# Chunk 4's scores in two steps, and the last weight pieces as halves through the scalar engine's queue: a fused attention and expert kernel on one Trainium2 core

## The chip, the cores and the metric

The kernel runs on one core of a Trainium2 chip. The core has a matrix engine (TensorE, PE in the rows), a vector engine (VectorE, DVE), a scalar engine (ScalarE, ACT), GpSimd (POOL), and a synchronisation engine (SyncE, SP) that here only starts transfers. ScalarE can start transfers as well. Each engine works through its own list of instructions in the order in which that list was written, and waits at the head of the list until what the instruction needs is there. The list of transfers that an engine starts is called its queue in this text. The metric is the time of one execution on the device in microseconds (us). Before the change it is 1141.03 us, the median of three runs (1140.71 to 1143.52).

## The reference, cut to what matters

Eight sequences of 576 tokens with 8 heads of 64 go through block-causal attention, and its output (4608 tokens by 512) through a two-layer expert with a gate. All is in float32; the two weight matrices come as 64-bit floats.

```python
scores = scale * np.matmul(q, k.transpose(0, 1, 3, 2))
mask = block_i >= block_j            # blocks of 64 positions
scores = np.where(mask, scores, -1000000000.0)
attn = np.exp(scores - np.max(scores, axis=-1, keepdims=True))
attn = attn / (np.sum(attn, axis=-1, keepdims=True) + 1e-09)
x = np.matmul(attn, v)               # then heads side by side: 4608 x 512
h = x @ w_in                         # 512 x 2048
g = h * (1.0 / (1.0 + np.exp(-1.702 * h)))
return (g @ w_out).astype(np.float32)   # 2048 x 512
```

## The kernel before, in words

**Turns.** Two heads make a pair, and 32 pairs give 32 turns, n = 0 to 31, and a last one. A turn scores pair n, multiplies pair n-1's weights with its values, and prepares pair n+1. The 576 rows of a pair are cut into five chunks, 0 to 4; chunk i has 64(2i+1) keys, so that chunk 4 is the widest with 576. What a turn does, and in which order, is written as a string of slots (lines 29 to 33, read by `order` and `step`). "3+0" scores chunks 3 and 0 side by side, "2+1" the next two, "4" the last. "V" multiplies the turned weights of the pair before with its values (`av`). "L" is `prep`: VectorE turns the loaded q and k of the next pair, and the loads for the pair behind that go out. B, C and a flip weights by TensorE in the first five turns only. After each slot, "-" too, weights are converted up to a quota and expert work goes out up to another quota. Turns 0 to 3 use FIRST, turn 4 START, turn 5 HANDOVER, turns 6 to 8 CONVERT and all later ones LATE.

**A pair's way.** `score` issues one product per chunk and head into a PSUM bank. `weigh` takes the bank with VectorE (line 349: mask, scale and row minimum in one instruction) and then ScalarE (line 356: the exponential with its sum). `normalise` makes the reciprocal on VectorE (lines 366 and 369) and scales the row on GpSimd (line 374). From turn 5 on `turn` transposes 32 by 32 blocks on VectorE into the tile `turned` (lines 383 and 388), and behind chunk 4 sixteen transfers on SP's queue (line 395) carry the blocks to the other partitions, from where `av` reads them. There is one copy of the source blocks and one of the target blocks: the next pair's transposes wait until the sixteen transfers have read, and the transfers wait until `av` has read.

**Banks.** [...] `bank` goes round the banks w0, w1 and w2 once the experts have begun, and from turn 9 on w3 as well. "3+0", "2+1" and "V" take two banks each. The order of TensorE's products is that of the source.

**Experts.** Tiles of 384 tokens go through 16 column groups fc of the hidden layer: 12 products into `hp`, the gate (lines 555, 556, 564 and 79), then 9 products of the group before into three accumulators. Tile 0 starts in turn 4, and its fc = 0 to 15 call for the weights as they go.

**Weights.** The 64-bit weights are split into a high and a low float32 part. There are 32 pieces of 128 rows by 512: for each of four column groups g, four pieces of w_in and then four of w_out. `load_weights` fetches a piece; `begin` turns the upper word by a ScalarE instruction into the bank w3 (line 213); `merge` takes the lower word on VectorE (lines 226 and 229) into `wm`, of which there is one; `split_weights` casts the high part on ScalarE (line 238) and subtracts on GpSimd (line 79). The first 28 pieces land in rooms that final weights will fill later. For the last four, all of w_out's group 3, no such room is left: each lands as two halves in the three buffers of the tag `osb`, which the output tiles use afterwards. `convert` runs a piece in two steps, `merge`, then `split_weights` and the next `begin`. The quota follows `WEIGHTS_BY` (position: pieces; position counts heads, two a turn), and the expert calls for a piece itself where the quota lags.

**Order.** All of this is the source's order. A planner reads it as priorities and writes each engine's list by its own estimate of durations; only TensorE's products and the first three weight loads are held to the order of the source.

The lines that the prediction's steps touch: 31 and 32 (the orders of turns 5 to 8), 36 (the quota), 184 to 202 (`load_weights`; its transfers all go through SP's queue, line 195), 208 to 239 (`begin`, `merge`, `split_weights`), 241 to 256 (`convert`), 303 to 336 (`score`), 395 (the sixteen transfers), 427 to 452 (`av`), and 536 (the expert's call for pieces).

Of the kernel before, what the change touches and what calls it, by code (L numbers as in the profile page):

```python
# [27 lines left out]

FIRST = "1+0 - B 2/3 - L C - 4 - V - a -"
START = "1+0 - B 2/3 C - V - 4 - a - L -"  # L30
HANDOVER = "B - C - 3+0 - V - 2+1 - - 4 - - L -"
CONVERT = "3+0 - 2+1 - - V - 4 - - - L - -"
LATE = "3+0/2+1 - - - - V - 4 - - - L -"


WEIGHTS_BY = ((0, 0), (8, 13), (14.5, 32))
TILES_BY = ((8.4, 0), (17, 1), (33.7, 4), (65.7, -2))


# [1 line left out]
def attention_moe_kernel(  # L41
# [29 lines left out]
    def f(ap):  # L71
        return ap.bitcast(F32)
# [38 lines left out]
    WC = 512  # L111
    NG = DF // WC
    FG = WC // P
    GROUP = NDC + FG

    def room(tag, shape, dt, name):
        return d2.tile(shape, dt, tag=tag, name=name, bufs=1)
# [44 lines left out]
    def width(i):  # L162
        return BLK * (2 * i + 1)
# [9 lines left out]
    for g in range(NG):  # L173
        for dc in range(NDC):
            src = wi64[dc * P : (dc + 1) * P, 2 * g * WC : 2 * (g + 1) * WC]
            pieces.append((src, "wi", g, dc))
        for fc in range(FG):
            r = (g * FG + fc) * P
            pieces.append((wo64[r : r + P], "wo", g, fc))

    places = [f"{n}{p}{g}" for n, g in (("wo", 3), ("wo", 2), ("wi", 3), ("wi", 2), ("wo", 3), ("wi", 3), ("wo", 3)) for p in "hl"]
    parts, pair_of = {}, {}

    def load_weights(upto):
        while conv["loaded"] < min(upto, len(pieces)):
            j = conv["loaded"]
            if j < 2 * len(places):
                if j % 2 == 0:
                    pair_of[j // 2] = room(places[j // 2], [P, 2, 2 * WC], U32, "words")
                at = [pair_of[j // 2][:, j % 2]]  # L190
            else:
                at = [d2.tile([P, WC], U32, tag="osb", name="wst", bufs=3) for _ in range(2)]
            n = 2 * WC // len(at)
            for x, w in enumerate(at):
                d = nc.sync.dma_start(out=w, in_=pieces[j][0][:, x * n : (x + 1) * n])
                if j < 3:
                    tc.keep_in_program_order(d)
            parts[j] = [
                (w.rearrange("p (c t) -> p c t", t=2), slice(x * n // 2, (x + 1) * n // 2))
                for x, w in enumerate(at)  # L200
            ]
            conv["loaded"] += 1


# [3 lines left out]
    def begin(j):  # L208


        bits[j] = ps.tile([P, 512], F32, tag="w3", name="wm")
        for w, c in parts[j]:
            nc.scalar.activation(
                out=bits[j][:, c], in_=f(w[..., 1]), func=AF.Prelu, scale=2.0**-112, alpha=-(2.0**32)
            )

    def merge(j):
        u = bits.pop(j).bitcast(U32)

        if j % 2 and j < 2 * len(places) - 4:  # L220
            z = d2.tile([P, WC], U32, tag="osb", name="wm", bufs=3)
        else:
            z = room("wm", [P, WC], U32, "wm")
        whole[j] = z
        for w, c in parts.pop(j):
            nc.vector.tensor_scalar(
                out=z[:, c], in0=w[..., 0], scalar1=29, scalar2=None, op0=ALU.logical_shift_right
            )
            nc.vector.scalar_tensor_tensor(
                out=z[:, c], in0=u[:, c], scalar=3, in1=z[:, c],  # L230
                op0=ALU.logical_shift_left, op1=ALU.bitwise_or,
            )

    def split_weights(j):
        _, name, g, x = pieces[j]
        z = whole.pop(j)
        hi, lo = (weights(name + p, g)[:, x] for p in "hl")
        nc.scalar.copy(out=hi, in_=f(z))  # L238
        subtract(nc.gpsimd, lo, f(z), f(hi))

    def convert(upto):

        while conv["step"] < int(2 * upto):
            j, odd = divmod(conv["step"], 2)
            if odd:
                split_weights(j)
                if j + 1 < len(pieces):
                    load_weights(min(j + 3, 2 * len(places) + 1))
                    begin(j + 1)
            else:  # L250
                if j == 0:
                    begin(0)
                merge(j)
                if j >= 2 * len(places):
                    load_weights(j + 2)
            conv["step"] += 1


    raw, qk = {}, {}
# [41 lines left out]
    stats = {}  # L301

    def score(n, banks):

        if n not in stats:
            mx = d2.tile([P, NCH + 1, 2], F32, tag="mx", name="mx")
            sm = d2.tile([P, NCH, 2], F32, tag="sm", name="sm")
            stats[n] = (mx, sm)
        todo = []
        for chunks in banks:  # L310

            part = []
            for lo, hi in ((0, 512),) if width(chunks[0]) <= 512 else ((0, 256), (256, S)):
                ss = [bank() for _ in range(2)]
                c = 0
                for i in chunks:
                    a, z = qrange(i)
                    w = min(hi, width(i)) - lo
                    for hd in range(2):
                        r = slice(hd * D, hd * D + D)  # L320

                        mm(
                            out=ss[hd][:, c : c + w], lhsT=qk[n][r, 0, a : a + P],
                            rhs=qk[n][r, 1, lo : lo + w], start=True, stop=True,
                        )
                        part.append((i, hd, lo, lo + w, ss[hd][0 : z - a, c : c + w]))
                    c += w
            todo.append(sorted(part, key=lambda x: (chunks[::-1].index(x[0]), x[2])))
        for chunks, part in zip(banks, todo):
            e = {}  # L330
            for i, hd, lo, hi, s in part:
                e[i] = weigh(n, i, hd, lo, hi, s, e.get(i))
            for i in chunks[::-1]:
                normalise(n, i, e[i])
                if not early(n):
                    turn(n, i, e[i])

    def weigh(n, i, hd, lo, hi, s, e):
        mx, sm = stats[n]
# [22 lines left out]
    def normalise(n, i, e):  # L362
        _, sm = stats[n]
        m = BLK if i == 0 else P
        c = sm[0:m, i]
        nc.vector.tensor_scalar(  # L366
            out=c, in0=c, scalar1=1e-9, scalar2=2.0, op0=ALU.add, op1=ALU.mult
        )
        nc.vector.reciprocal(out=c, in_=c)  # L369
# [94 lines left out]
    def step(n):  # L464

        turns["n"] = n
        now = n < NPAIR

        def item(x):
            if x == "V":  # L470
                return (lambda: av(n - 1)) if n else None
            if x == "L":
                return (lambda: prep(n + 1)) if n + 1 < NPAIR else None
            if x in ("a", "B", "C"):
                m, chunks = {"a": (n, [0, 1]), "B": (n - 1, [2, 3]), "C": (n - 1, [4])}[x]
# [33 lines left out]
    def moe():  # L509
# [17 lines left out]
        for t in range(NT):  # L527
# [5 lines left out]
            acc = [ps.tile([P, DM], F32, tag=f"acc{c}", name=f"acc{c}") for c in range(tt // P)]  # L533
            for fc in range(NFC):
                if t == 0:
                    convert(fc // FG * GROUP + NDC + fc % FG + 1)
                hp = ps.tile([P, 512], F32, tag="h", name="hp")
                fs = slice(fc % FG * P, (fc % FG + 1) * P)
                terms = [(wa, xb, dc) for dc in range(NDC) for wa, xb in (("wih", xh), ("wil", xh), ("wih", xl))]
# [112 lines left out]
```

## Time and profile before

| what | value |
|---|---|
| median of three runs | 1141.03 us (1140.71 to 1143.52) |
| the profiled execution: its own time | 1139.9 us |
| its span, first to last instruction | 1138.1 us (1.8 us of the time lie around it) |
| TensorE busy in the span | 1076.8 us (95%) |
| VectorE, ScalarE, GpSimd busy | 580.2, 487.6, 409.6 us |
| turns 5 to 8 | from about 96 to 234 us of the span |
| TensorE busy from 96 to 234 us | 112.5 of 138 us |
| TensorE busy from 420 to 980 us | about 99% |

In a row of the timeline stand the start, the duration, engine, line, operation, tiles and count, and in brackets the time for which the engine sat idle before it, with what released it. A row of the waits has who waited for whom, then the total, the number of times and the longest. "SPq" is a transfer in SP's queue; its duration is the time it takes to be issued, not to land. PEclk is the clock granted to TensorE in tenths of full speed.

### The profile page before, as it was taken

The page shows a single profiled execution, that of the slowest core. Times are in us where ns is not written, and L with a number is a line of the kernel's source. Part 1 is how long each engine was busy: PE and PEld are TensorE (multiplying, and loading weights), DVE is VectorE, ACT ScalarE, POOL GpSimd, SP SyncE. Part 2 cuts the span into 40 slices and gives each one's busy share as a digit, 9 for nine tenths or more (in the row PEclk, how much of TensorE's full clock was granted, in tenths as well). Part 3 has the DMA queues.
Part 4 walks back from the last instruction along what each step waited for, and adds up shares of the span by engine and source line. Part 5 has one row for each costly group of instructions (what it writes and reads, how often), then busy time and mean ns, then how long its engine had stood idle before and what let it go on. Part 6 is the DMA issues. An engine that isn't in the chain of part 4 may idle for free. (4 is left out here: it accounts for less than half of the span.)

```text
span 1138.1 us, 19868 instructions
## 1 busy us (share of the span) xinstructions
PE 1076.8 (95%) x6870; PEld 910.4 (80%) x6870; DVE 580.2 (51%) x1863; ACT 487.6 (43%) x1291; POOL 409.6 (36%) x509
## 2 busy tenths in 40 slices
PE   5879796899999999999999999999999999999998
PEld 3658574788788888888888888888888888899997
DVE  6766765645555655554555655455555564211211
ACT  5866543533343444443443443343443344232322
POOL 5665644333233333333333233332332333222222
PEclk8979899899999999999999999999999999999999
DMA  8653363443343343343343333343333332200000
GB/s 173 196 143 91 106 174 78 103 102 84 73 101 75 69 99 67 78 112 81 77 106 72 70 90 65 84 111 74 84 97 69 70 90 56 53 29 1 29 1 28
DMA packets 221668, 95.66 MB, mean 84 GB/s; under 512 B 198528, under 2 KB 198528, under 8 KB 221568
## 3 DMA queue, kind: packets, MB, share of 16 engines
q1 hardware_dynamic: 216832, 93.81, 35.0%
q10 hardware_dynamic: 4736, 0.59, 0.3%
q8 instruction: 54, 0.88, 0.3%
q14 instruction: 46, 0.38, 0.1%
HBM read 45.09 MB, written 9.44 MB: 48 GB/s over the span
## 5 line engine op out<-in xcount | busy, mean ns | idle before, releaser
L79 POOL TENSOR_TENSOR gl<-g,gh 128x384 fp32r<-128x384 f32 x192 | 195.3, 1017 | 542.3 <-ACT gh L564 449.6
L96 PE MATMUL hp<-xh,wih 128*128 128x384 f32 x768 | 266.1, 346 | 11.0 <-DVE g L556 10.3
L556 DVE SCALAR_TENSOR_TENSOR g<-g,hp 128x384 f32<-128x384 f32 x192 | 105.6, 550 | 329.6 <-ACT g L555 328.4
L96 PE MATMUL hp<-xh,wil 128*128 128x384 f32 x768 | 260.1, 339 | 0.0
L96 PE MATMUL hp<-xl,wih 128*128 128x384 f32 x768 | 254.8, 339 | 0.0
L555 ACT ACTIVATE g<-hp 128x384 f32<-128x384 f32 x192 | 94.2, 491 | 349.7 <-PE hp L96 343.0
L96 PE MATMUL acc<-woh,gh 128*128 128x512 f32 x576 | 232.6, 404 | 3.5 <-ACT woh L238 3.5
L96 PE MATMUL acc<-wol,gh 128*128 128x512 f32 x576 | 228.7, 397 | 0.6 <-POOL wol L79 0.6
L96 PE MATMUL acc<-woh,gl 128*128 128x512 f32 x576 | 228.0, 396 | 0.5 <-POOL gl L79 0.5
L356 ACT ACTIVATE e<-e,mx 64x64 f32<-64x64 f32 (+1 forms) x270 | 148.9, 553 | 80.1 <-DVE mx L349 80.1
L374 POOL TENSOR_TENSOR e<-e,sm 128x448 f32<-128x448 f32 (+4 forms) x222 | 135.6, 631 | 129.2 <-DVE sm L369 76.0
L96 PEld LDWEIGHTS hp<-xh,wih 128*128 128x128 f32 x768 | 145.5, 189 | 35.4 <-DVE g L556 22.3
L564 ACT CAST gh<-g 128x384 fp32r<-128x384 f32 x192 | 98.5, 513 | 156.1 <-DVE g L556 155.9
L96 PEld LDWEIGHTS hp<-xh,wil 128*128 128x128 f32 x768 | 145.7, 190 | 6.9 <-issue 0.2
L96 PEld LDWEIGHTS hp<-xl,wih 128*128 128x128 f32 x768 | 145.0, 189 | 0.4 <-DVE xl L79 0.4
L96 PE MATMUL bank<-qk 64*128 64x320 f32 (+4 forms) x768 | 123.7, 430 | 20.7 <-DVE mx L349 9.3
L96 PEld LDWEIGHTS acc<-woh,gh 128*128 128x128 f32 x576 | 108.7, 189 | 34.2 <-issue 9.9
L383 DVE STREAM_TRANSPOSE turned<-e 128x384 f32<-128x384 f32 (+1 forms) x216 | 104.4, 500 | 62.0 <-POOL e L374 56.6
L96 PEld LDWEIGHTS acc<-wol,gh 128*128 128x128 f32 x576 | 108.6, 189 | 24.6 <-POOL wol L79 1.1
L96 PEld LDWEIGHTS bank<-qk 64*128 64x128 f32 x768 | 70.6, 194 | 65.0 <-issue 30.1
L96 PEld LDWEIGHTS acc<-woh,gl 128*128 128x128 f32 x576 | 108.8, 189 | 17.2 <-POOL gl L79 1.4
L349 DVE CUSTOM_DVE_ANT_0 e<-bank,mask 64x64 f32<-64x64 f32 (+2 forms) x270 | 99.5, 417 | 29.2 <-PE bank L96 25.6
(48 smaller groups left out, 865.9 us busy)
## 6 DMA issues: line engine op xcount, KB each, us to landing
turned<-turned SPq DMA_DIRECT2D x216, 80.0 KB, 2.1
turned<-turned SPq DMA_DIRECT2D x108, 112.0 KB, 2.2
turned<-turned SPq DMA_DIRECT2D x108, 88.0 KB, 2.1
raw<-in_q_dram SPq DMA_DIRECT2D x128, 72.0 KB, 2.4
out_dram<-osb SPq DMA_DIRECT2D x36, 256.0 KB, 2.3
raw<-in_k_dram SPq DMA_DIRECT2D x120, 72.0 KB, 2.4
words<-in_moe_w_in_dram SPq DMA_DIRECT2D x16, 512.0 KB, 6.3
vp<-in_v_dram SPq DMA_DIRECT2D x60, 128.0 KB, 2.4
```

The source lines that it names most:

```text
L79: eng.tensor_tensor(out=out, in0=in0, in1=in1, op=ALU.subtract)
L96: return tc.keep_in_program_order(nc.tensor.matmul(**kw))
L349: nc.vector.tensor_tensor_reduce(out=e[0:m, hd, lo:hi], in0=s, in1=mk, op0=ALU.add, op1=ALU.min, scale=-0.125, scalar=3e38 if lo == 0 else ...
L356: nc.scalar.activation(out=e[0:m, hd], in_=e[0:m, hd], func=AF.Exp, scale=-1.0, bias=mx[0:m, i, hd : hd + 1], accum_out=sm[0:m, i, hd : hd ...
L374: nc.gpsimd.tensor_tensor(out=x, in0=x, in1=sc.to_broadcast([m, width(i)]), op=ALU.mult)
L383: nc.vector.transpose(out=tw[:, :, SLOT[i] : SLOT[i] + i, hd].rearrange("p b j c -> p j b c"), in_=e[:, hd, 0 : i * P],)
L555: nc.scalar.activation(out=g, in_=hp[:, 0:tt], func=AF.Tanh, scale=1.702)
L556: nc.vector.scalar_tensor_tensor(out=g, in0=g, scalar=1.0, in1=hp[:, 0:tt], op0=ALU.add, op1=ALU.mult)
L564: nc.scalar.copy(out=gh, in_=g)
```

## The change

Four things change together.

- **Chunk 4 in two steps** ("l" and "h"). In turns 5 to 8 "l" scores chunk 4's keys 0 to 256, with two banks, and "h" the keys 256 to 576 with two more. Two slots of expert work lie between them. Between the steps the half-weighed row is kept in `begun`; exponential, scaling, transposes and transfers follow "h".
- **The orders.** In turn 5 "V" moves from slot 7 to slot 6 of 16, "2+1" from 9 to 7, "4" at slot 12 becomes "l" at 9 and "h" at 11, and "L" goes from 15 to 12. In turns 6 to 8 "V" moves from slot 6 to 5 of 14, "4" at slot 8 becomes "l" at 7 and "h" at 9, and "L" goes from 12 to 11.
- **Halves as pieces.** Each of the last four pieces becomes two pieces of 128 rows by 256, with a `begin`, `merge` and `split_weights` of their own. There are 36 pieces now. The first three halves are loaded when pieces 26 and 27 are split, the other five as soon as a buffer is free, three ahead.
- **Their queue.** The first three halves go through SP's queue, the other five through ScalarE's.

`WEIGHTS_BY` is rewritten for 36 pieces; `needed` tells for the expert which pieces a column group calls for.

```diff
-HANDOVER = "B - C - 3+0 - V - 2+1 - - 4 - - L -"
-CONVERT = "3+0 - 2+1 - - V - 4 - - - L - -"
+HANDOVER = "B - C 3+0 - V 2+1 - l - h L - - - -"
+CONVERT = "3+0 - 2+1 - V - l - h - L - - -"
...
-WEIGHTS_BY = ((0, 0), (8, 13), (14.5, 32))
+WEIGHTS_BY = ((0, 0), (8, 13), (13.2, 28), (14.6, 36))
...
-            pieces.append((wo64[r : r + P], "wo", g, fc))
+            n = 1 if g < NG - 1 else 2
+            for x in range(n):
+                c = slice(x * WC // n, (x + 1) * WC // n)
+                pieces.append((wo64[r : r + P, 2 * c.start : 2 * c.stop], "wo", g, fc, c))
...
+    NW = 2 * len(places)
     def load_weights(upto):
...
-                at = [d2.tile([P, WC], U32, tag="osb", name="wst", bufs=3) for _ in range(2)]
-            n = 2 * WC // len(at)
-            for x, w in enumerate(at):
-                d = nc.sync.dma_start(out=w, in_=pieces[j][0][:, x * n : (x + 1) * n])
+                w = d2.tile([P, WC], U32, tag="osb", name="wst", bufs=3)
+            d = (nc.sync if j < NW + 3 else nc.scalar).dma_start(out=w, in_=pieces[j][0])
...
     def convert(upto):
...
                 split_weights(j)
                 if j + 1 < len(pieces):
-                    load_weights(min(j + 3, 2 * len(places) + 1))
+                    load_weights(j + 3 if j < NW - 2 else max(NW + 3, j + 4))
                     begin(j + 1)
             else:
                 if j == 0:
                     begin(0)
                 merge(j)
-                if j >= 2 * len(places):
-                    load_weights(j + 2)
+    def needed(fc):
+        g, x = divmod(fc, FG)
+        return 1 + max(j for j, y in enumerate(pieces) if y[2] == g and (y[1] == "wi" or y[3] == x))
...
-    def score(n, banks):
+    def score(n, banks, keys=None):
...
-            for lo, hi in ((0, 512),) if width(chunks[0]) <= 512 else ((0, 256), (256, S)):
+            for lo, hi in keys or (((0, 512),) if width(chunks[0]) <= 512 else ((0, 256), (256, S))):
...
-            e = {}
+            e = begun
             for i, hd, lo, hi, s in part:
                 e[i] = weigh(n, i, hd, lo, hi, s, e.get(i))
             for i in chunks[::-1]:
+                if part[-1][3] < width(part[-1][0]):
+                    continue
                 normalise(n, i, e[i])
                 if not early(n):
                     turn(n, i, e[i])
+                e.pop(i)
...
+            if x in ("l", "h"):
+                return (lambda: score(n, [[NCH - 1]], [{"l": (0, 256), "h": (256, S)}[x]])) if now else None
...
-                    convert(fc // FG * GROUP + NDC + fc % FG + 1)
+                    convert(needed(fc))
```

More of the change, by code (lines that the diff above doesn't have):

```diff
@@ L113, in attention_moe_kernel @@
     FG = WC // P
-    GROUP = NDC + FG
     def room(tag, shape, dt, name):
@@ L175, in attention_moe_kernel @@
             src = wi64[dc * P : (dc + 1) * P, 2 * g * WC : 2 * (g + 1) * WC]
-            pieces.append((src, "wi", g, dc))
+            pieces.append((src, "wi", g, dc, slice(0, WC)))
         for fc in range(FG):
             r = (g * FG + fc) * P
-            pieces.append((wo64[r : r + P], "wo", g, fc))
+            n = 1 if g < NG - 1 else 2
+            for x in range(n):
+                c = slice(x * WC // n, (x + 1) * WC // n)
+                pieces.append((wo64[r : r + P, 2 * c.start : 2 * c.stop], "wo", g, fc, c))
     places = [f"{n}{p}{g}" for n, g in (("wo", 3), ("wo", 2), ("wi", 3), ("wi", 2), ("wo", 3), ("wi", 3), ("wo", 3)) for p in "hl"]
-    parts, pair_of = {}, {}
+    NW = 2 * len(places)
+    words, pair_of = {}, {}
     def load_weights(upto):
@@ L186, in load_weights @@
             j = conv["loaded"]
-            if j < 2 * len(places):
+            if j < NW:
                 if j % 2 == 0:
                     pair_of[j // 2] = room(places[j // 2], [P, 2, 2 * WC], U32, "words")
-                at = [pair_of[j // 2][:, j % 2]]
+                w = pair_of[j // 2][:, j % 2]
             else:
-                at = [d2.tile([P, WC], U32, tag="osb", name="wst", bufs=3) for _ in range(2)]
-            n = 2 * WC // len(at)
-            for x, w in enumerate(at):
[L195 to L201, printed above, removed]
+                w = d2.tile([P, WC], U32, tag="osb", name="wst", bufs=3)
+            d = (nc.sync if j < NW + 3 else nc.scalar).dma_start(out=w, in_=pieces[j][0])
+            if j < 3:
+                tc.keep_in_program_order(d)
+            words[j] = w.rearrange("p (c t) -> p c t", t=2)
             conv["loaded"] += 1
@@ L208, in begin @@
     def begin(j):
[L211 to L215, printed above, removed]
+        n = pieces[j][4].stop - pieces[j][4].start
+        bits[j] = ps.tile([P, 512], F32, tag="w3", name="wm")[:, 0:n]
+        nc.scalar.activation(
+            out=bits[j], in_=f(words[j][..., 1]), func=AF.Prelu, scale=2.0**-112, alpha=-(2.0**32)
+        )
     def merge(j):
         u = bits.pop(j).bitcast(U32)
-        if j % 2 and j < 2 * len(places) - 4:
+        w = words.pop(j)
+        if j % 2 and j < NW - 4:
             z = d2.tile([P, WC], U32, tag="osb", name="wm", bufs=3)
@@ L223, in merge @@
             z = room("wm", [P, WC], U32, "wm")
[L224 to L232, printed above, removed]
+        z = whole[j] = z[:, 0 : u.shape[1]]
+        nc.vector.tensor_scalar(
+            out=z, in0=w[..., 0], scalar1=29, scalar2=None, op0=ALU.logical_shift_right
+        )
+        nc.vector.scalar_tensor_tensor(
+            out=z, in0=u, scalar=3, in1=z, op0=ALU.logical_shift_left, op1=ALU.bitwise_or
+        )
     def split_weights(j):
-        _, name, g, x = pieces[j]
+        _, name, g, x, c = pieces[j]
         z = whole.pop(j)
-        hi, lo = (weights(name + p, g)[:, x] for p in "hl")
+        hi, lo = (weights(name + p, g)[:, x, c] for p in "hl")
         nc.scalar.copy(out=hi, in_=f(z))
@@ L299, in prep @@
             load(m)
-    stats = {}
-    def score(n, banks):
+    stats, begun = {}, {}
+    def score(n, banks, keys=None):
         if n not in stats:
```

## The prediction

> **What bounds the kernel now.** I read the page first, then TensorE's busy time by stretch, then its timeline where it idles, then the lists that hold it up there. The first fence has the span and TensorE's forty slices from the page, the second two stretches.
>
> ```profile
> span 1138.1 us, 19868 instructions
> ...
> PE   5879796899999999999999999999999999999998
> ```
>
> ```profile
> 420.00:980.00 560.00, 555.53 (x3625) 473.63 (x3624) 303.14 (x998) 231.16 (x625) 186.97 (x241) 1.00 0.37 83
> 96.00:234.00 138.00, 112.50 (x686) 91.02 (x685) 85.87 (x260) 66.37 (x172) 67.31 (x74) 0.91 0.46 117
> ```
>
> From slice 8 on TensorE is never short of work: 555.5 us busy of 560. Nothing saved on another engine counts there, and a microsecond that TensorE stops losing earlier is a microsecond off the end. In turns 5 to 8 it is busy 112.5 of 138 us (the first number behind the length; VectorE, ScalarE and GpSimd follow with 85.9, 66.4 and 67.3 behind PEld's). So 25.5 us are open there, and no engine is full. The timeline of TensorE shows where:
>
> ```profile
> 106.77 2.98 PE L96 MATMUL bank<-turned,vp 128*64 128x128 f32 x60
> ...
> 115.85 1.23 PE L96 MATMUL bank<-qk 64*128 64x256 f32 x6
> 121.25 1.43 PE L96 MATMUL bank<-qk 64*128 64x320 f32 x2 [4.17 <-DVE mx L349]
> ...
> 143.32 4.63 PE L96 MATMUL bank<-turned,vp 128*64 128x128 f32 x60 [5.00 <-DMA turned<-turned]
> ...
> 151.39 0.80 PE L96 MATMUL bank<-qk 64*128 64x320 f32 x2 [0.16 <-DVE mx L349]
> ...
> 165.54 1.10 PE L96 MATMUL bank<-qk 64*128 64x320 f32 x6 [1.15 <-DVE mx L349]
> ...
> 169.90 2.87 PE L96 MATMUL bank<-turned,vp 128*64 128x128 f32 x56
> 175.76 0.34 PE L96 MATMUL bank<-turned,vp 128*64 128x64 f32 x4 [2.99 <-DVE mx L349]
> ...
> 183.69 0.80 PE L96 MATMUL bank<-qk 64*128 64x320 f32 x2 [3.80 <-DVE mx L349]
> ...
> 196.74 0.50 PE L96 MATMUL acc<-woh,gh 128*128 128x512 f32 x1 [3.51 <-ACT woh L238]
> ...
> 198.10 0.80 PE L96 MATMUL acc<-wol,gh 128*128 128x512 f32 x1 [0.63 <-POOL wol L79]
> ...
> 211.30 4.64 PE L96 MATMUL bank<-turned,vp 128*64 128x128 f32 x60 [3.53 <-DMA raw<-in_q_dram]
> ...
> 246.46 2.98 PE L96 MATMUL bank<-turned,vp 128*64 128x128 f32 x60
> ```
>
> The rows with x60 (and x56 with x4) are V of turns 5, 6, 7, 8 and 9, at 106.77, 143.32, 169.90, 211.30 and 246.46. The waits shown add up to 24.9 us: for chunk 4's own bank 4.17, 0.16 and 3.80; for a bank of "2+1" 1.15 and 2.99; for the last weights 3.51 and 0.63; for the turned blocks 5.00 and 3.53 (the second is put down to another transfer of the same queue). A long wait costs twice: behind 5.00 and 3.53 the sixty products of V take 4.63 and 4.64 us, against 2.98 where nothing was waited for, another 1.65 each; the two products at 121.25 take 1.43 against 0.80, 0.6 more. With these 3.9 us the sum is 28.8.
>
> V waits for the sixteen transfers of chunk 4. So I followed SP's queue, the timeline and then its longest wait for a weight buffer:
>
> ```profile
> 131.47 10.14 SPq L395 DMA_DIRECT2D turned<-turned  x16
> ...
> 157.60 10.09 SPq L395 DMA_DIRECT2D turned<-turned  x16
> ...
> 174.37 1.73 SPq L195 DMA_DIRECT2D wst<-in_moe_w_out_dram  x3
> ...
> 176.62 0.51 SPq L287 DMA_DIRECT2D vp<-in_v_dram  x1
> 194.69 0.92 SPq L195 DMA_DIRECT2D wst<-in_moe_w_out_dram  x2
> ...
> 198.45 0.33 SPq L195 DMA_DIRECT2D wst<-in_moe_w_out_dram  x1
> 199.13 10.07 SPq L395 DMA_DIRECT2D turned<-turned  x16
> ```
>
> ```profile
> SPq L195 <- DVE wm L226: 18.9, 2, 17.1
> ```
>
> The sixteen take 10.1 us to be issued, and V starts 11.9 us (131.47 to 143.32), 12.3 and 12.2 us behind the first. Turns 5 to 8 are thus a ring: V, "4", weighing, transposes, 12.2 us of transfers, next V. From V(6) to V(7) it took 26.6 us, 14.3 of them from V to the first transfer. From V(7) to V(8) it took 41.4. There SP stood 17.1 us in front of a half piece whose buffer VectorE had not yet read out, and the sixteen were behind it. VectorE's list shows that their blocks had long been ready:
>
> ```profile
> 120.77 0.42 DVE L349 CUSTOM_DVE_ANT_0 e<-bank,mask 128x256 f32<-128x256 f32 x1
> ...
> 122.72 0.55 DVE L349 CUSTOM_DVE_ANT_0 e<-bank,mask,mx 128x320 f32<-128x320 f32 x1
> ...
> 126.48 0.55 DVE L556 SCALAR_TENSOR_TENSOR g<-g,hp 128x384 f32<-128x384 f32 x1 [1.28 <-ACT g L555]
> 126.95 0.16 DVE L369 RECIPROCAL sm<-sm 128x2 f32<-128x2 f32 x1
> ...
> 190.25 0.31 DVE L388 STREAM_TRANSPOSE turned<-e 64x128 f32<-64x128 f32 x1
> ```
>
> The last transpose of turn 7 ended at 190.56, the first transfer went out at 199.13: 8.6 us for the queue alone.
>
> **The change, part by part.** I follow the four Vs, since they are the ring's beat; TensorE's work in a turn is shorter than the beat. That work comes from the chain that ended last:
>
> ```profile
> 973.69 2.10 PE hp L96 x12
> 975.80 2.08 PE acc L96 x9
> ```
>
> A group of the expert takes 4.18 us. One tile of 16 groups is spread over positions 8.4 to 17, so 3.7 groups or 15.6 us fall to a turn, 1.1 us to a slot of 14 and 0.97 to a slot of 16. V adds 2.98, and the 24 score products some 4.4, at the 1.10 us for six in the row of 165.54. That is 23 us a turn.
>
> *Two steps for chunk 4, turn 5.* No instruction is added: eight products, eight minima as before. "h" asks for its second bank 0.97 x 2 us after "l", where "4" asked at once and waited 4.17. The wait falls away, but V(6) hangs on the transfers, not on TensorE. What counts is when chunk 4's row is done. VectorE reached the first minimum at 120.77, 4.9 us behind the first products at 115.85, held by transposes and weight merges that stay in its list; the last minimum at 122.72 waited for the product of 121.25, and the reciprocal at 126.95 stood behind the gate instruction of 126.48, which waited for the expert's products that the 4.17 had pushed back. The bounds: 0.5 us if VectorE's list alone decides, 8 us if the minima come the full 4.9 us sooner and the reciprocal loses its 3 us behind the gate. I take 5.5, nearer the upper one, since V, "2+1" and the first step all stand one to three slots earlier. V(6) comes to 137.8.
>
> *Turn 6.* Here "4" hardly waited (0.16), so its split only delays: V to "4" was two slots, V to "h" is four. That is 2.2 us less 0.16, so 2.0 us more on the ring: 28.6 in place of 26.6. "L" comes two slots behind "h" where it stood four behind "4", and its eight loads may now be issued ahead of the sixteen; by the row below that is 8 x 0.5 = 4 us on SP, at worst 2 of which the 3 us of scaling and transposing would not cover. So the ring's bounds are 26.6 (VectorE is late anyway) and 30.6. V(7) comes to 137.8 + 28.6 = 166.4.
>
> ```profile
> L276 SPq DMA_DIRECT2D raw<-in_q_dram x128: 311/497/1532, 0.7 to 916.8; - x128
> L276 ACTq DMA_DIRECT2D raw<-in_k_dram x8: 317/371/577, 0.7 to 6.0; - x8
> L213 ACT ACTIVATE wm<-words x28: 604/631/671, 13.0 to 165.3; 128x512 f32<-128x512 f32 x28
> L213 ACT ACTIVATE wm<-wst x8: 378/394/417, 170.6 to 201.2; 128x256 f32<-128x256 f32 x8
> ```
>
> *The queue and the halves, turn 7.* Eight half transfers stay eight. Three go through SP into free buffers; five go through ScalarE, at 0.37 us each by the only transfers it issued (second row), 1.9 us in all. Each waits for a merge that the cast ahead of it in ScalarE's list waits for anyway. `begin` and `merge` were halves already; the four casts and four subtractions become eight and eight. A half costs 0.62 of a whole (0.394 to 0.631), so a pair costs a quarter more, about one instruction of each kind in all; ScalarE and GpSimd, busy half the time (66 and 67 of 138 us), cover it. Then SP has no weight in front of the sixteen, and the ring runs at 28.6 instead of 41.4. Against that stands the end of the conversion: TensorE reaches column groups 12 to 15 some 14 us sooner than when it waited 4.1 us for them. The halves are fetched three ahead, so I take 2 us of waiting, between 0 and the 5 us that the old wait and what it slowed cost. V(8) comes to 166.4 + 28.6 + 2 = 197.0 instead of 211.3.
>
> [...]
>
> *Turn 8 and after.* V(9) waited for nothing: its sixteen had been issued well before 246.46. V stands a slot earlier in turn 8, so from V(8) to V(9) there are 1.1 us more of the expert's work. Everything later only moves up.
>
> The sum: V(8) is 14.3 us sooner, less 1.1, so 13.2. The profiled execution took 1139.9 us (its span and 1.8), which gives 1126.7; the median of the runs is 1.1 above that execution, so 1128. By the bounds (turn 5 0.5 to 8, ring 26.6 to 30.6 twice, weights 0 to 5) the saving is 0.5 - 4.0 + 5.7 - 1.1 = 1.1 at the least and 8 + 14.8 - 1.1 = 21.7 at the most: 1119 to 1140.
>
> **The rivals.** *All waits but V's first go.* If VectorE and GpSimd, with TensorE never stalled, weigh faster, the ring falls below TensorE's 23 us in turns 6 and 7. Then of the 28.8 only the 5.00 + 1.65 before V(6) stay: 22 us saved, 1119. For it: no engine is full. Against it: 12.2 us of transfers and 14.3 before them in the one undisturbed turn.
>
> *The queue gives only its issue time.* SP's wait was a symptom: merges of the last weights came late on VectorE, behind turn 7's transposes, and if the planner writes the lists so again, the sixteen are late in another way. Then turn 5's 5.5, less 2.0, plus 1.8 stay: 5 us, 1136. Against it: the 8.6 us between 190.56 and 199.13.
>
> *ScalarE takes over the blocked queue: slower.* Behind a transfer that waits on ScalarE stand the exponentials and the gate (lines 356, 555, 564), and TensorE has one `hp` bank that the gate must empty. On SP such a wait lasted 17.1 us. If the planner puts one of the five ahead of work that does not depend on its merge, and the merge again comes after turn 7's transposes, those 17.1 us fall on TensorE, with 1.9 us of issue: 1128 + 19 = 1147. It decides against the change from a hold of 13.2 us on, and it is slower by what can be measured from 17. Against it: the cast in front waits for the same merge.
>
> *The change does not do what it says.* "h" still waits for the bank of "l" because VectorE is 4.9 us behind, and V takes the rest: about 1140.
>
> **How the numbers follow.** Forecast 0.55, the faster rival 0.12, issue time only 0.15, ScalarE blocked 0.11, nothing done 0.07. A change within 0.3% (3.4 us) can't be told from none here. Faster holds the forecast, the faster rival and two thirds of the third (1136 lies 5 us below 1141): 0.77. Slower is 0.11 and a little for what no row shows: 0.12. The same is 0.11. The range takes in the bounds, the faster rival and no change: 1115 to 1141, which leaves the slower rival out and some of what lies beyond the bounds.
>
> **What would show it.** Step 1 is right if the two wide products of "h" wait under 1 us in turns 5 and 7. Step 2: V(6) and V(7) still wait for transfers, and the ring is 28 to 29 us. Step 3: in turn 7 the sixteen start within 1 us of the last transpose, and no weight row of SP waits. Step 4: the last casts are done before TensorE asks, to within 2 us. The prediction is wrong if V(5) to V(8) isn't 85 to 100 us long (104.5 before), or if ScalarE stands over 3 us in front of a transfer.

## The result, and the profile after

The changed kernel takes 1149.0 us in the median of 4 runs (1147.46 to 1150.28), against 1141.82 us for the kernel before on the same chips (4 runs, 1140.71 to 1143.52). The ratio is 1.0061 with a 95% interval of 1.0042 to 1.0080: slower, by about 7 us, where 1128 us was forecast. The profiled execution took 1150.28 us.

The page of the changed kernel, its span and TensorE's forty slices, and the two stretches of the prediction (behind the length: PE, PEld, VectorE, ScalarE, GpSimd busy, each with its count, then the granted clock of TensorE, the DMA share and GB/s):

```profile
span 1148.4 us, 19884 instructions
...
PE   6869886799999999999999999999999999999998
```

```profile
420.00:980.00 560.00, 554.45 (x3627) 471.39 (x3622) 308.22 (x1014) 233.24 (x630) 186.65 (x241) 1.00 0.36 81
96.00:234.00 138.00, 109.49 (x653) 87.59 (x652) 83.23 (x251) 64.18 (x173) 69.34 (x78) 0.85 0.45 112
```

The long stretch is as before (554.5 of 560 us busy), so the loss lies ahead of it. From 96 to 234 us TensorE does less, 109.5 in place of 112.5 us, at a granted clock of 0.85 in place of 0.91. TensorE's timeline shows its new waits (start, length, instruction, and in brackets the idle time ahead with what ended it):

```profile
110.73 2.99 PE L96 MATMUL bank<-turned,vp 128*64 128x128 f32 x60
...
118.06 0.85 PE L96 MATMUL bank<-qk 64*128 64x256 f32 x4
...
125.93 1.43 PE L96 MATMUL bank<-qk 64*128 64x320 f32 x2 [4.18 <-DVE mx L353]
...
151.27 5.27 PE L96 MATMUL bank<-turned,vp 128*64 128x128 f32 x60 [4.74 <-DMA turned<-turned]
...
183.70 4.45 PE L96 MATMUL bank<-turned,vp 128*64 128x128 f32 x60 [3.07 <-DMA turned<-turned]
...
195.88 1.22 PE L96 MATMUL bank<-qk 64*128 64x256 f32 x2 [4.12 <-ACT xr L453]
...
222.39 5.53 PE L96 MATMUL bank<-turned,vp 128*64 128x128 f32 x60 [7.57 <-DMA turned<-turned]
...
257.90 2.98 PE L96 MATMUL bank<-turned,vp 128*64 128x128 f32 x60
```

V of turns 5 to 9 starts at 110.73, 151.27, 183.70, 222.39 and 257.90. V(5) to V(8) is 111.7 us long; it was 104.5. The 7.1 us of difference is as much as the medians differ (7.2). SP's list shows the sixteen transfers of the three turns:

```profile
139.47 10.14 SPq L399 DMA_DIRECT2D turned<-turned  x16
172.03 10.06 SPq L399 DMA_DIRECT2D turned<-turned  x16
...
210.22 10.31 SPq L399 DMA_DIRECT2D turned<-turned  x16
```

From such rows each turn of the ring can be cut in three: from V's first product to the end of chunk 4's last minimum, from there to the first of the sixteen, and from there to the next V. The third part takes 11.7 to 12.3 us in both kernels, so the first two tell the story (us; turn 8 whole only):

| kernel | turn 5 | turn 6 | turn 7 | turn 8 | median |
|---|---|---|---|---|---|
| before | 36.55 (16.50, 8.20) | 26.58 (9.46, 4.82) | 41.40 (15.18, 14.05) | 35.16 | 1141.8 |
| forecast | 31.05 | 28.6 | 30.6 | 36.3 | 1128 |
| after | 40.54 (17.41, 11.33) | 32.43 (12.29, 8.47) | 38.69 (19.17, 7.35) | 35.51 | 1149.0 |

Turn 7 did become shorter, but by 2.7 us and not by 10.8; turns 5 and 6 lost 4.0 and 5.9.

Two lists explain this. VectorE's in turn 5 (L353 the minimum, L562 the gate, L370 the step that readies the row's sum, called the sum from here on, L373 the reciprocal, L392 the last transpose), and from ScalarE's the second exponential of chunk 4:

```profile
125.45 0.42 DVE L353 CUSTOM_DVE_ANT_0 e<-bank,mask 128x256 f32<-128x256 f32 x1
...
127.59 0.55 DVE L353 CUSTOM_DVE_ANT_0 e<-bank,mask,mx 128x320 f32<-128x320 f32 x1
...
128.66 1.43 DVE L296 STREAM_TRANSPOSE qk<-raw 128x576 f32<-128x576 f32 x2
133.18 0.55 DVE L562 SCALAR_TENSOR_TENSOR g<-g,hp 128x384 f32<-128x384 f32 x1 [3.09 <-ACT g L561]
133.65 0.16 DVE L370 TENSOR_SCALAR sm<-sm 128x2 f32<-128x2 f32 x1
```

```profile
128.71 0.77 ACT L360 ACTIVATE e<-e,mx 128x576 f32<-128x576 f32 x1
129.37 0.20 ACT L360 ACTIVATION_READ_ACCUMULATOR e<-e,mx 128x1 f32 x1
```

Chunk 4's exponentials were done at 129.57, but its sum ran at 133.65, 4.1 us later: the planner had written it behind the expert's gate, which waited 3.09 us. In the kernel before, the sum had stood ahead of the gate (126.48), and only the reciprocal behind it:

```profile
124.56 0.32 DVE L366 TENSOR_SCALAR sm<-sm 128x2 f32<-128x2 f32 x1
```

GpSimd then had a subtraction of the weights (L79) in front of the first of the two scalings (L378) for which the transposes waited; the gate's subtraction between the two had stood there before as well:

```profile
133.74 1.56 POOL L79 TENSOR_TENSOR wol<-wm,woh 128x512 fp32r<-128x512 f32 x1 [4.89 <-ACT woh L236]
135.25 1.14 POOL L378 TENSOR_TENSOR e<-e,sm 128x576 f32<-128x576 f32 x1
136.36 1.01 POOL L79 TENSOR_TENSOR gl<-g,gh 128x384 fp32r<-128x384 f32 x1
137.33 1.32 POOL L378 TENSOR_TENSOR e<-e,sm 128x576 f32<-128x576 f32 x1
```

In turn 7 the sixteen start together with the last transpose (210.22), but that transpose is late. The same two lists there:

```profile
193.72 0.33 ACTq L197 DMA_DIRECT2D wst<-in_moe_w_out_dram  x1
...
194.80 0.40 ACT L212 ACTIVATE wm<-wst 128x256 f32<-128x256 f32 x1
195.14 0.20 ACT L452 COPY xr<-bank 128x64 f32<-128x64 f32 x1
195.24 0.58 ACT L453 COPY xr<-bank 128x512 f32<-128x512 f32 x1
```

```profile
201.22 0.29 DVE L225 TENSOR_SCALAR wm<-wst 128x256 uint32<-128x256 uint32 x1 [1.28 <-POOL wol L79]
201.51 0.55 DVE L353 CUSTOM_DVE_ANT_0 e<-bank,mask,mx 128x320 f32<-128x320 f32 x1
...
202.33 0.54 DVE L353 CUSTOM_DVE_ANT_0 e<-bank,mask,mx 128x320 f32<-128x320 f32 x1
...
210.22 0.31 DVE L392 STREAM_TRANSPOSE turned<-e 64x128 f32<-64x128 f32 x1
```

ScalarE copies V's result out of its banks (xr) only at 195.24, behind four of the half pieces; the second half of "l" wants one of those banks and waits 4.12 us. So "h" comes late, at 200.67, and its wide minima stand behind merges that wait for GpSimd.

### The profile page after: what moved, and what is told of

It reads as the page before. It is cut to its first block, busy times and chain, and to the rows that moved or that the text cites. A ratio compares the mean times of both kernels' runs of the same rounds, so it can differ in the third digit from the quotient of the medians.

```text
span 1148.4 us, 19884 instructions
## 1 busy us (share of the span) xinstructions
PE 1081.7 (94%) x6870; PEld 915.3 (80%) x6870; DVE 580.4 (51%) x1863; ACT 488.3 (43%) x1295; POOL 410.8 (36%) x513
## 5 line engine op out<-in xcount | busy, mean ns | idle before, releaser
L79 POOL TENSOR_TENSOR gl<-g,gh 128x384 fp32r<-128x384 f32 x192 | 195.2, 1017 | 547.2 <-ACT gh L570 452.1
L96 PE MATMUL hp<-xh,wih 128*128 128x384 f32 x768 | 267.3, 348 | 11.9 <-DVE g L562 11.2
L562 DVE SCALAR_TENSOR_TENSOR g<-g,hp 128x384 f32<-128x384 f32 x192 | 105.4, 549 | 329.8 <-ACT g L561 328.7
L360 ACT ACTIVATE e<-e,mx 64x64 f32<-64x64 f32 (+2 forms) x270 | 148.8, 552 | 83.3 <-DVE mx L353 83.3
L378 POOL TENSOR_TENSOR e<-e,sm 128x448 f32<-128x448 f32 (+4 forms) x222 | 136.2, 633 | 130.0 <-DVE sm L373 69.9
L353 DVE CUSTOM_DVE_ANT_0 e<-bank,mask 64x64 f32<-64x64 f32 (+2 forms) x270 | 99.5, 417 | 28.6 <-PE bank L96 24.7
```

The costliest lines, as they stand in the source:

```text
L79: eng.tensor_tensor(out=out, in0=in0, in1=in1, op=ALU.subtract)
L96: return tc.keep_in_program_order(nc.tensor.matmul(**kw))
L353: nc.vector.tensor_tensor_reduce(out=e[0:m, hd, lo:hi], in0=s, in1=mk, op0=ALU.add, op1=ALU.min, scale=-0.125, scalar=3e38 if lo == 0 else ...
L360: nc.scalar.activation(out=e[0:m, hd], in_=e[0:m, hd], func=AF.Exp, scale=-1.0, bias=mx[0:m, i, hd : hd + 1], accum_out=sm[0:m, i, hd : hd ...
L562: nc.vector.scalar_tensor_tensor(out=g, in0=g, scalar=1.0, in1=hp[:, 0:tt], op0=ALU.add, op1=ALU.mult)
```

## The experiments

All kernels compute the whole result. Ratios are against the kernel before, of the runs on the same chip; its median there is 1141.8 to 1142.4 us.

**One part at a time.** `weights_alone` is the changed kernel with the old orders, so that chunk 4's scores come in one step again:

```
-HANDOVER = "B - C 3+0 - V 2+1 - l - h L - - - -"
-CONVERT = "3+0 - 2+1 - V - l - h - L - - -"
+HANDOVER = "B - C - 3+0 - V - 2+1 - - 4 - - L -"
+CONVERT = "3+0 - 2+1 - - V - 4 - - - L - -"
```

> The halves as pieces, their queue and the new weight quota, with the orders and the single step of chunk 4 of before. Theory A (the new order of scores lengthens the ring of turns 5 and 6, the weights part is sound): in turn 7 the sixteen transfers start within 1 us of the last transpose, the ring of turn 6 stays near 26.6 us, and the time is 1131 to 1138 us. Theory B (the half pieces in ScalarE's and VectorE's lists cost more than the queue gives): turn 7 stays at 38 us or more and the time is 1142 to 1148 us.

`steps_alone` is the kernel before with the two new orders and the code for "l" and "h", and nothing of the weights.

> The two steps and the new orders alone, weights and queue as before. Theory A: 1148 to 1156 us, the ring of turn 6 near 32 us, and SP still stands over 5 us in front of a half piece in turn 7. Theory B: 1138 to 1143 us, since the steps then cost little.

Measured: `weights_alone` 1134.32 us (1133.43 to 1134.6), ratio 0.9923 (0.9908 to 0.9938), 8.0 us faster. `steps_alone` 1144.73 us (1142.99 to 1146.28), ratio 1.0019 (1.0008 to 1.0029), about 2 us slower; that falls between the two theories' ranges.

| kernel | turn 5 | turn 6 | turn 7 | V(5) to V(8) |
|---|---|---|---|---|
| weights_alone | 36.58 (16.52, 8.20) | 26.71 (9.60, 4.83) | 34.73 (13.95, 6.63) | 98.0 |
| steps_alone | 40.26 (16.91, 11.54) | 32.59 (12.45, 8.46) | 36.39 (13.52, 10.72) | 109.2 |
| after | 40.54 (17.41, 11.33) | 32.43 (12.29, 8.47) | 38.69 (19.17, 7.35) | 111.7 |

The losses of turns 5 and 6 belong to the steps with their orders. Turn 7 gains with either part, 6.7 us with the weights and 5.0 with the steps. Added up, the medians alone would give -8.0 + 2.4 = -5.6 us; together the parts cost 7.2. Of the 12.8 us between, 9.0 show in turn 7 (41.40 - 6.67 - 5.01 = 29.72 against 38.69). Some 4 of these are no loss but a gain that can't be had twice: each part alone shortens the way from the last minimum to the first transfer, where SP's queue had stood (14.05 to 6.63 and to 10.72). The rest is mostly the part up to the last minimum, which grows to 19.17 from 13.95 or 13.52. The other 3.8 us are what the medians and V(5) to V(8) of single profiles differ by.

In `weights_alone` V(8) no longer waits for the transfers. TensorE loses 4.20 us ahead of turn 8's "3+0" instead, for the next pair's turned q and k. And ScalarE's halves still touch SP's queue: one of the sixteen of turn 7 waits for a half that ScalarE issued (SP's waits; more under `queue_alone`):

```profile
SPq L399 <- DMA wst<-in_moe_w_out_dram: 1.4, 1, 1.4
```

**Is it the step's lateness or the split?** `one_step_early` is the changed kernel with "4" whole where "l" stands:

```
-HANDOVER = "B - C 3+0 - V 2+1 - l - h L - - - -"
-CONVERT = "3+0 - 2+1 - V - l - h - L - - -"
+HANDOVER = "B - C 3+0 - V 2+1 - 4 - - L - - - -"
+CONVERT = "3+0 - 2+1 - V - 4 - - - L - - -"
```

> The changed kernel, but chunk 4 in one step at the slot of its first step; V, the other scores, L and the weights stand as changed. Theory C (distance: the second step stands two slots later behind V, so the row is done later): in turn 6 from V to the first of the sixteen transfers it takes about 18 us instead of 20.8, and the time is 1141 to 1145 us. Theory D (lists: sum and reciprocal of chunk 4 stand behind the gate and the weights in VectorE's list, whatever the step): about 20 us, and 1147 us or more.

Measured: 1139.52 us (1135.54 to 1142.09), ratio 0.9962 (0.9942 to 0.9982). That is below theory C's 1141 to 1145, and from V to the first transfer turn 6 takes 14.5 us, not 18. Turn 6 is back at 26.57 (9.87, 4.67), turn 5 at 37.22 (18.36, 7.07). Its VectorE in turn 6:

```profile
156.74 0.55 DVE L353 CUSTOM_DVE_ANT_0 e<-bank,mask,mx 128x320 f32<-128x320 f32 x1
...
158.41 0.17 DVE L370 TENSOR_SCALAR sm<-sm 128x2 f32<-128x2 f32 x1 [0.42 <-ACT e L360]
158.62 0.17 DVE L373 RECIPROCAL sm<-sm 128x2 f32<-128x2 f32 x1
...
161.85 0.52 DVE L562 SCALAR_TENSOR_TENSOR g<-g,hp 128x384 f32<-128x384 f32 x1
```

With the scores in one step the sum comes ahead of the gate. So the unfavourable order of turn 6 goes with the second step, four slots after V where "4" had stood two after it; it is no property of the new orders as such. Whether it is the split or the lateness isn't separated: no run has "4" whole at the slot of "h". The new orders cost something too: `one_step_early` differs from `weights_alone` by them alone and is 5.2 us slower (1139.52 against 1134.32, though its six runs spread over 6.5 us), 2.0 of it in turn 7 (36.75 against 34.73).

**What the order is worth.** `sum_first` keeps both steps and adds edges that only order the lists of VectorE and GpSimd (no wait between engines): in turns 5 to 8 the gate, the merges and the preparation's transposes go behind chunk 4's reciprocal, the subtractions behind its scaling.

```
+    def behind(ins, eng):
+        if eng in first:
+            tc.add_manual_dep(ins.ins, first[eng].ins.name, <order only>)
+        return ins
...
+        rc = nc.vector.reciprocal(out=c, in_=c)
+        if i == NCH - 1 and EARLY <= n <= 2 * HP: first["D"] = rc
```

> The changed kernel, with VectorE's gate, weight merges and L's transposes listed behind chunk 4's reciprocal, and GpSimd's subtractions behind chunk 4's scaling, in turns 5 to 8, wherever the source has them later; nothing else differs. Theory D: in turn 6 from V to the first transfer 17 us or less instead of 20.8, in turn 5 the reciprocal no longer waits for the gate, and the time is 1136 to 1143 us. Theory C: the distance behind V stays, so 19 us or more and 1146 to 1150 us.

Measured: 1139.82 us (1138.4 to 1140.46), ratio 0.9973 (0.9962 to 0.9985): 9.2 us less than the changed kernel. From the last minimum to the first transfer turn 5 takes 6.75 in place of 11.33, turn 6 5.20 in place of 8.47. From V to the first transfer turn 6 takes 17.9 us, between the two theories; the time is theory D's. In turn 5:

```profile
124.91 0.55 DVE L364 CUSTOM_DVE_ANT_0 e<-bank,mask,mx 128x320 f32<-128x320 f32 x1
...
126.93 0.17 DVE L381 TENSOR_SCALAR sm<-sm 128x2 f32<-128x2 f32 x1 [0.85 <-ACT e L371]
127.13 0.17 DVE L384 RECIPROCAL sm<-sm 128x2 f32<-128x2 f32 x1
...
130.41 0.55 DVE L578 SCALAR_TENSOR_TENSOR g<-g,hp 128x384 f32<-128x384 f32 x1 [2.44 <-ACT g L577]
```

The way to the last minimum stays nearly as long as in the changed kernel (16.42, 12.71 and 19.07 us, against 17.41, 12.29 and 19.17), so turn 6's 3 us and turn 7's 5 us there have another cause.

**The halves in turn 7.** `late_halves` is the changed kernel with the due point of the last pieces moved by one position: `(14.6, 36)` becomes `(15.6, 36)`.

> The changed kernel with one number changed: the halves fall due from position 13.2 to 15.6 instead of 14.6, so two fewer stand ahead of chunk 4's minima in turn 7. Theory G (in turn 7 the two steps and the halves get in each other's way on ScalarE and VectorE: 19.2 us from V to the last minimum, against 13.5 and 14.0 with either alone): 15 to 17.5 us, the wait of 4.1 us for the copy of V's result is under 2, and the time is 1144 to 1147 us. If the two steps alone make turn 7 long: 19 us and 1148 to 1150 us.

Measured: 1141.33 us (1138.71 to 1142.3), ratio 0.9988 (0.9978 to 0.9999), 7.7 us less than the changed kernel and below theory G's 1144 to 1147: the interference that G names is there and larger. Turn 7 is 33.26 (16.07, 4.83) in place of 38.69. ScalarE's copy of V's result starts 6.0 us after V in place of 11.5 (187.65 behind 181.62 against 195.24 behind 183.70), behind two of its five half transfers and not four; in `weights_alone` it comes ahead of all five, 6.6 us after V. The 4.12 us wait for it is gone. So in turn 7 the halves' casts and transfers, in ScalarE's list in front of the copy, made most of what both parts together cost beyond either alone: in the changed kernel "h" comes 17.0 us after V, in `steps_alone` 11.7, here 11.2. What is left of the 5 us here is the merges in VectorE's list: from "h" to the last minimum it takes 4.9 us, in `steps_alone` 1.9.

**The queue and the halves apart.** `halves_on_sp` is `weights_alone` with every half on SP's queue; `queue_alone` is the kernel before with its eight half transfers on ScalarE's queue and nothing else.

```
-            d = (nc.sync if j < NW + 3 else nc.scalar).dma_start(out=w, in_=pieces[j][0])
+            d = nc.sync.dma_start(out=w, in_=pieces[j][0])
```

> As weights_alone (orders and single step of before, the last weights as halves three ahead), but all eight halves go through SP's queue. Theory E (the gain is that no weight transfer stands in front of the sixteen): SP waits for a half's buffer again, the sixteen of turn 7 start more than 3 us behind the last transpose, and the time is 1138 to 1142 us instead of 1134. Theory F (the gain comes from fetching three ahead and from finer pieces, whichever queue): the sixteen start within 1 us of the last transpose and the time is 1133 to 1136 us.

```
-                d = nc.sync.dma_start(out=w, in_=pieces[j][0][:, x * n : (x + 1) * n])
+                d = (nc.sync if j < 2 * len(places) else nc.scalar).dma_start(out=w, in_=pieces[j][0][:, x * n : (x + 1) * n])
```

> The kernel before, with only the eight half transfers of the last four pieces moved to ScalarE's queue; whole pieces, orders and the single step stay. Theory E: turn 7's sixteen start within 1 us of the last transpose, from V to V in turn 7 it takes 33 to 37 us instead of 41.4, and the time is 1134 to 1138 us. Theory F: the merges of the last weights stay as late as before, turn 7 stays above 39 us and the time is 1140 to 1144 us; if ScalarE stands in front of a transfer for long, it is more.

`halves_on_sp` takes 1139.99 us (1136.13 to 1142.1), ratio 0.9972 (0.9956 to 0.9987). SP again stands in front of halves, and behind it the sixteen start at 197.48, 6.8 us after the last transpose ended (190.41 + 0.31). SP's longest wait in 160 to 200 us of this kernel (in total, times, longest):

```profile
SPq L197 <- DVE wm L225: 14.9, 5, 8.3
```

So pieces in halves bring some 2 us by themselves, and taking the last five off SP another 5.7 (1139.99 to 1134.32).

`queue_alone` takes 1146.95 us (1146.26 to 1147.17), ratio 1.0041 (1.0026 to 1.0056): slower than before, which I hadn't expected. At a transfer and the cast behind it ScalarE stands at most 3.8 us. Turn 7 does fall, with the sixteen at the last transpose as theory E had it, and to 27.22 us, below its 33; but turns 5 and 6 lose 4.9 and 14.4. It is SP that stands, in the middle of the sixteen of turn 6 (its timeline, and its waits from 160 to 210 us):

```profile
163.55 23.83 SPq L395 DMA_DIRECT2D turned<-turned  x16
```

```profile
SPq L395 <- DMA wst<-in_moe_w_out_dram: 14.0, 2, 12.3
```

The sixteen take 23.83 us to be issued in place of 10.09, with waits for half transfers of the other queue, whose data they don't touch. Why they wait for them isn't shown. The longest wait is 12.3 us; ScalarE issues the first two of its last five halves only at 178.98, 15.4 us behind the first of the sixteen. The sixteen of turn 5 are held too, at 14.81 us in place of 10.14.

`queue_on_gpsimd` is `queue_alone` with `nc.gpsimd` for `nc.scalar`.

> The kernel before with its eight half transfers moved to GpSimd's queue in place of ScalarE's. In queue_alone (1146.95 us) the sixteen transfers of turn 6 took 23.83 us to be issued in place of 10.07, with 14.0 us of waits for half transfers that stand on ScalarE. [...] Then the sixteen of turn 6 take 10 to 10.5 us, no row of SP waits for a half, V(6) to V(7) is 26 to 29 us, and V(5) to V(8) 94 to 102; GpSimd issues eight transfers, so the time is 1131 to 1139. Theory T: a second queue itself (its transfers running beside the sixteen, or the halves arriving late) holds the sixteen back. Then they take over 18 us again, V(6) to V(7) stays above 35, and the time is 1144 to 1149.

Measured: 1143.95 us (1142.04 to 1145.2), ratio 1.0015 (1.0006 to 1.0024). The sixteen of turn 6 are issued in 10.06 us without a wait for a half, within the 10 to 10.5 us expected and against theory T's 18, and V(6) to V(7) is 26.9 us. So the hold came with ScalarE's queue and not with a second queue as such. But the time is 5 us above the range of 1131 to 1139. In turn 7 a new wait takes what was won (SP's timeline, TensorE's, VectorE's):

```profile
160.02 10.06 SPq L395 DMA_DIRECT2D turned<-turned  x16
```

```profile
190.18 0.48 PE L96 MATMUL bank<-turned,vp 128*64 128x64 f32 x4 [14.99 <-DVE mx L349]
```

```profile
174.71 1.21 DVE L226 TENSOR_SCALAR wm<-wst 128x256 uint32<-128x256 uint32 x2 [2.42 <-POOL wil L79]
...
178.70 0.29 DVE L226 TENSOR_SCALAR wm<-wst 128x256 uint32<-128x256 uint32 x1 [2.11 <-POOL wol L79]
...
182.79 0.50 DVE L226 TENSOR_SCALAR wm<-wst 128x256 uint32<-128x256 uint32 x2 [1.69 <-POOL wol L79]
...
185.98 0.29 DVE L226 TENSOR_SCALAR wm<-wst 128x256 uint32<-128x256 uint32 x1 [2.03 <-POOL wol L79]
...
187.90 1.03 DVE L383 STREAM_TRANSPOSE turned<-e 128x384 f32<-128x384 f32 x2
189.07 0.36 DVE L349 CUSTOM_DVE_ANT_0 e<-bank,mask 128x192 f32<-128x192 f32 x1
```

V's last four products wait 14.99 us for a bank of "2+1", whose minima come at 189.07, behind the merges of the last four pieces: with the old handling a piece goes round VectorE, ScalarE and GpSimd before the next merge can start (the four L226 rows, each behind a subtraction of GpSimd). So in the kernel before the blocked queue was one face of a chain of late pieces. Freed there, it blocks VectorE; cut into halves but left on SP, it blocks the queue again, for less. The halves alone pay some 2 us and another queue alone nothing; both together (`weights_alone`) pay 8.

**Versions.** `weights_sum_first` is `weights_alone` with the edges of `sum_first`; `weights_late_sum_first` has the later due point (15.6) as well; `steps_late_sum_first` is the changed kernel with both repairs, so against the second it differs by the steps alone.

> weights_alone, with the list order of sum_first: in turns 5 to 8 gate, weight merges and L's transposes behind chunk 4's reciprocal on VectorE, and GpSimd's subtractions behind its scaling. If the list order is worth as much with one step as with two (1.4 to 4.6 us in turns 5 and 6 there), turn 5's 8.2 us from the last minimum to the first transfer fall to about 6, turn 6's 4.8 stay, and the time is 1130 to 1133 us. If the gate's delay costs TensorE as much, 1133 to 1137.

> weights_sum_first (1132.92 us, one step for chunk 4) with the due point of the last pieces moved from position 14.6 to 15.6. If the halves' casts and merges are what lengthens turn 7 (theory G, by late_halves, where turn 7 came to 33.26 from 38.69), turn 7 goes from 32.8 to 29 to 31 and the time to 1129 to 1131. If turn 7 here is already free of them (theory H), the due point only brings the last weights late: turn 7 stays at 32 to 34, TensorE waits 2 us or more for weights behind it, and the time is 1133 to 1136.

> The changed kernel, two steps for chunk 4, with both repairs: chunk 4's sum and scaling ahead of the gate, merges and preparation, and the due point of the last pieces at 15.6. Against weights_late_sum_first it differs by the steps alone. The prediction's step 1 (the split brings V(6) 5.5 us sooner) with step 2 (turn 6 2 us later) would make it 3 us faster than that kernel: 1126 to 1128. Theory A (the second step comes later than the whole of chunk 4 came before; turn 5 gains 1 to 2 us, turns 6 and 7 lose 2 to 4 each) makes it 1 to 6 us slower: 1131 to 1136.

| kernel | median us (runs) | ratio (95%) | turns 5, 6, 7 |
|---|---|---|---|
| weights_sum_first | 1132.92 (1129.36 to 1134.09) | 0.9914 (0.9896 to 0.9933) | 33.35, 28.08, 32.80 |
| weights_late_sum_first | 1132.10 (1130.34 to 1133.73) | 0.9917 (0.9901 to 0.9934) | 34.00, 26.97, 34.43 |
| steps_late_sum_first | 1134.10 (1133.44 to 1136.01) | 0.9933 (0.9918 to 0.9948) | 35.40, 29.85, 33.90 |

The first two beat both kernels, by 9 to 10 us against the one before, and can't be told from each other, nor well from `weights_alone`: with one step the order was mostly right already, and turn 7 holds no halves in front of the copy, so theory G's 29 to 31 us for turn 7 didn't come (34.43, near H's 32 to 34, with a time between their ranges). With both repairs, as theory A had it, the steps with their orders are still about 2 us slower than one step (four runs each, whose ranges just touch), and turn 5 takes 35.40 us against 34.00. That they are worth something, as the prediction's first step has it, doesn't hold in any setting tried.

## Why the prediction was wrong

The frame held. In the changed kernel and the eleven experiments the length of V(5) to V(8) differs from that of before by the change of the median, to within 2.5 us (after +7.1 and +7.2; `weights_alone` -6.5 and -8.0; `queue_alone` +5.1 and +4.5; `queue_on_gpsimd`, 107.50 to 215.37, +3.3 and +2.0). Step by step:

**"Two steps for chunk 4, turn 5" failed, and it decides the sign.** It took V(6) 5.5 us sooner, out of 0.5 to 8; measured is 4.0 later, outside the bounds. Three things in it were wrong. The wait of 4.17 us for the second bank did not go away but moved: 4.18 before the second half of "h" (125.93). The products did come sooner after V (7.3 us for "l", 118.06 behind 110.73, against 9.1 for "4"), but the first minimum did not (125.45, 14.7 us after V against 14.0): VectorE's list decided, the case I had put at the lower bound. And the reciprocal's 3 us behind the gate, which I counted as won, became 4.1 for the sum: with the stall in place the gate came later still (5.0 us behind the end of the last minimum, 3.2 before), and the planner now put the sum behind it too. The order of the list was taken as given, with only a gain in it; `sum_first` shows what it cost, 5.6 us in turn 5 (40.54 to 34.97) and 9.2 in the whole. A bound below nothing was missing. The step also counts "eight minima" for chunk 4; VectorE's list has four, which changes nothing in the sum.

**"Turn 6"**: 2.0 us more were forecast, 5.9 came. Of these 2.8 are the distance of "h" (9.46 to 12.29 up to the last minimum), which is the 2.2 forecast a little undersized; the other 3.65 are the order again (4.82 to 8.47), and `sum_first` gives 3.3 of them back; the transfers take 0.6 less. The clause on "L" ahead of the sixteen played no part that the runs show, and its bound was a sum gone wrong: 4 us of loads less 3 covered leave 1 and not 2.

**"The queue and the halves, turn 7"** was right in its mechanism and its size was off. No weight row of SP waits, and the sixteen start at the last transpose. Alone, this part brings turn 7 from 41.40 to 34.73 and the kernel 8.0 us. But the forecast counted the bigger number of casts as covered by engines that are half busy. They are covered in busy time, not in order: beside the steps they stand in front of the copy and the minima and stretch the way to the last minimum from 13.95 to 19.17. That is the term that was mis-sized, at 0 where it measured 5.2; `late_halves` gives 3.1 of it back.

**"Turn 8 and after"**: 1.1 us more forecast, 0.35 measured.

The rivals. "The queue gives only its issue time" put the planner's lists at the centre, and was nearest to what the lists did, though at the wrong place; as a statement on the queue it fails in the changed kernel and holds in another form for the queue alone. Its 1.8 us for the issue of five transfers no run shows: taking five off SP was worth 5.7 us beside pieces in halves (`halves_on_sp` against `weights_alone`), and moving all eight with the pieces whole cost 4.5 (`queue_alone`). "ScalarE takes over the blocked queue" named a time of 1147, close to 1149, for a reason that occurred in small only: no half stood on ScalarE over 3 us, but the copy of V's result came behind four of them, and TensorE waited 4.12 us for it. That its time came near is mostly luck: the larger loss was VectorE's order. "The change does not do what it says" was half true, since "h" waited as "4" had.

By its own marks: step 1 is wrong in turn 5 (4.18 against under 1); step 2 is right that V(6) and V(7) wait for transfers and wrong on the ring (32.4 against 28 to 29); step 3 is right; so is step 4, no product waits for the last weights; V(5) to V(8), at 111.7, is outside 85 to 100.

What stays open: in the profile of the changed kernel V(5) itself starts 4.0 us later, at 110.73 in place of 106.77. One us of that belongs to the change: in turn 5 "3+0" also moved, from slot 5 to 4 (the diff has it, the list of the orders doesn't), and ahead of it TensorE waits 1.5 us for copies of flipped weights in all six kernels with the new order and 0.5 in the seven with the old one. The rest goes with that execution: 1.5 us are there by 80 us, and from 80 to 90 us its granted clock was 0.61, against 1.00 in that of the kernel before. From 80 to 82 us the expert's products of 384 columns took 0.52 us there, and mostly 0.33 or 0.34 in the kernel before and in five experiments (`weights_alone`, `late_halves`, `queue_on_gpsimd`, `weights_late_sum_first`, `steps_late_sum_first`). Why the clock fell there isn't tested. The runs don't tell either why the planner moves the sum behind the gate when the second step is later, only that it does.

## What to carry to other kernels

Before counting a stall as removed, look at what stands next to it in the list of the engine that is late: where a planner writes the lists, moving one step by two slots can put a 0.2 us instruction 4 us behind its input, and an order-only edge is the cheap test. An engine that is half idle hides added work only if nothing urgent is queued behind it (in the changed kernel ScalarE was busy 64.2 of 138 us, and the way to turn 7's last minimum took 19.17 us against 13.95 in `weights_alone`). A transfer moved to another queue can still hold up the old one (1.4 us in `weights_alone`, 14.0 in `queue_alone`), and the move gains nothing if the work behind the transfer is the real chain (2.0 us slower in `queue_on_gpsimd`).

## What the runs showed of the hardware

With the halves on ScalarE's queue (`queue_alone`), SP's sixteen transfers of turn 6 took 23.83 us to be issued in place of 10.09, with 14.0 us of waits for halves whose data they don't use; with the halves on GpSimd's (`queue_on_gpsimd`) they took 10.06, without such a wait. In the changed kernel TensorE's sixty products of V took 4.45 to 5.53 us behind waits of 3.07 to 7.57 us, and 2.98 without, as before the change.
